# Nearest code by one minimum over 32-bit words of distance and rank

## The chip, the cores and the metric

The kernel runs on one core of a Trainium2 chip. The metric is the device time of one execution in microseconds (us). A core has five engines with instruction queues of their own, each of which works in order: PE (TensorE, matrix multiplication; PEld is its loading of weights), DVE (VectorE), ACT (ScalarE), POOL (GpSimd) and SP (SyncE, which here issues DMAs). [...]

## The reference

A three-tap convolution along time, a SiLU, four stages of residual vector quantisation with eight code words each, and a second three-tap convolution over the sum of the chosen words:

```python
B, T, D, K = 2, 16000, 512, 3
Nq, C = 4, 8
z = sum(xp[:, i:i+T, :] * dw_enc[i] for i in range(K))     # bfloat16
res = silu(z)
for s in range(Nq):
    cb = codebooks[s]
    d2 = |res|^2 - 2 res.cb + |cb|^2                        # [B, T, C]
    idx = d2.argmin(-1)
    sel = cb[idx]
    q = q + sel
    res = res - sel
y = sum(qp[:, i:i+T, :] * dw_dec[i] for i in range(K))
```

`argmin` takes the first of equal distances. The distances are bfloat16, so equal ones do occur, and the kernel has to break ties by the index.

## The kernel before

The 32,000 tokens are cut into 250 groups of 128 tokens (token p*250+g is row p of group g). The groups are worked in 16 chunks: one of 12 groups, fourteen of 16 and one of 14 (`SIZES`, L25). A chunk goes through these steps:

- **load** (L348): one transposing DMA for each group and its two neighbours brings x into XT, with the 512 features on the partitions in four blocks of 128. SP issues it (L358). There are two XT buffers. The first chunk comes another way (`load_rows`, L319), through PE transposes and four moves by ACT and DVE (L335, L337).
- **front** (L383): for each of the four blocks, `product` multiplies by the three taps (L410, into one Z and two T tiles), `total` adds them (L418), then ACT computes exp (L422), DVE adds one (L426), ACT computes the logarithm (L430) and exp (L433), and DVE writes the product into RES (L438). There are three Z tiles, three T tiles and three RES buffers.
- **stage** (L469), four times: PE scores the tokens in three banks of 5 or 6 groups (L489, L494). DVE takes the squared norm as a maximum (L502, TR) and copies the eight dot products (L505, PR). Then comes a tail of six small DVE instructions on 128 partitions x 16 groups x 8 codes, once for each stage and chunk, 64 times in all, each reading what the one before wrote: `with_norm` (L522, V), `distance` (L528, D2), `least` (L532, the minimum M over the eight codes), `marks` (L536: is the distance equal to the minimum?), `first` (L541, the maximum M2) and `onehot` (L549, OH). PE transposes OH (L559), ACT copies it out of PSUM (L566), PE multiplies it with the negated code words (L584), and the result is added to RES by DVE (L596) or, together with a copy of RES through PE (L601), by ACT (L607). How many of the four blocks go by DVE is the list `ON_DVE`.
- **finish** (L664): PE decodes from the four one-hot codes (L633), ACT moves the result out (L639, YSB, three buffers) and SP stores it (L643).

A KEY buffer is a tile of 32-bit words, also viewed as pairs of bfloat16. Before the first use `presets` (L269) writes the rank C-c into the lower half of every word of each of the three buffers, by eight memsets for each (L271). `marks` writes 1 or 0 into the upper half; among the words with a 1 the float32 maximum is then the one with the highest rank, which is the lowest code index. `presets` also clears the OH buffer (L272).

The order on each engine comes from a planner, `Plan` (L40). Every step is a task with an engine, a hold and a delay (assumed costs in us), the tasks that it needs, a due time, and the slots (buffers) that it takes and gives. The planner plays the program through: whenever an engine is free, the ready task with the earliest due time whose slots are there goes next, and its instructions are emitted in that order. Real waits are then set by semaphores that follow the actual reads and writes. In the plan a chunk's XT slot is given back when the third product of the fourth block is done (`give=("XT",)`, L452); the products need only the load. The tail's six tasks stand at L570 to L575 with holds of 0.2, 0.15, 0.2, 0.2, 0.2 and 0.2 us, the presets at L298 with 0.8 us, and the task with `taps_of`, which clears a decoder table on DVE and loads it through POOL's queue (L286, L288), at L303.

Of the kernel before, what the change touches and what calls it, by code (L numbers as in the profile page):

```python
# [10 lines left out]
BF16 = mybir.dt.bfloat16  # L11
F32 = mybir.dt.float32
ALU = mybir.AluOpType
ACT = mybir.ActivationFunctionType
AX = mybir.AxisListType
# [3 lines left out]
GC = 16  # L19
J = 4  # L20
# [99 lines left out]
def kernel(  # L120
# [8 lines left out]
    nc = tc.nc  # L129
    P = nc.NUM_PARTITIONS  # L130
    B, T, D = x.shape
    K = dw_enc.shape[0]
    Nq, C, _ = codebooks.shape
    KT = D // P
# [9 lines left out]
    const = ctx.enter_context(tc.tile_pool(name="const", bufs=1))  # L144
# [5 lines left out]
    small = ctx.enter_context(tc.tile_pool(name="small", bufs=3))  # L150
# [31 lines left out]
    for i in range(KT):  # L182
# [3 lines left out]
    free = {"RES": [], "KEY": [], "OH": []}  # L186
    plan = Plan({"XT": 2, "Z": ZB, "T": TB, "E": EB, "LN": LNB, "Y": YB, "psG": 2, "psD": 2, "psA": 2, "RES": 3, "KEY": 3,
                 "OH": 3})

    RESB = []  # L190
    for n in range(3):
        t = const.tile([P, KT, 2 * GC, NC + HT], BF16, name=f"RES{n}")
# [5 lines left out]
    G = chunks[0]["G"]  # L198
# [4 lines left out]
    for b in range(B):  # L203
        p = b * HB
# [58 lines left out]
    for n in range(3):  # L263
        t = const.tile([P, GC, C], F32, name=f"KEY{n}")
        free["KEY"].append((t, t.rearrange("p g c -> p (g c)").bitcast(BF16).rearrange("p (g c h) -> p g c h", c=C, h=2)))
        t = const.tile([P, GC, Nq, C], BF16, name=f"OH{n}")
        free["OH"].append(t)

    def presets(n):  # L269
        for c in range(C):  # L270
            nc.vector.memset(KEYS[n][1][:, :, c, 0], float(C - c))  # L271
        nc.vector.memset(OHB[n], 0.0)  # L272

    KEYS, OHB = list(free["KEY"]), list(free["OH"])

# [1 line left out]
    for name, first, tap, count in (("A0", 0, 1, 2), ("A1", 0, 0, 3), ("A2", 1, 0, 3), ("A3", 2, 0, 2),  # L279
                                    ("B0", 3, 0, 1), ("B3", 0, 2, 1), ("A2LO", 1, 0, 1)):  # L280
        t = const.tile([P, D], BF16, name=name)
# [16 lines left out]
    preset = [plan.add("DVE", 0.8, 1.0, [], early + 2.0 if n == 0 else 0.1 * PERIOD, lambda n=n: presets(n)) for n in range(3)]  # L298
# [3 lines left out]
    for n, name in enumerate(PARTS):  # L302
        t = plan.add("DVE", 0.2, 6.0, [], (0.3 + 0.02 * n) * PERIOD, lambda name=name: taps_of(name))  # L303
# [79 lines left out]
    def front(st, org):  # L383
        n, G, MB = st["n"], st["GP"], st["MB"]
        f = G / GC

        def dve(full):
            return 0.1 + (full - 0.1) * f

        def act(full):  # L390
            return 0.2 + (full - 0.2) * f


        def taps(i, k):
            return st["XT"][:, i, k:k + G, :].rearrange("p (m j) t -> p j m t", j=J)

        def places(t):
            return t[:, 0:G, :].rearrange("p (j m) t -> p j m t", m=MB)

        def halves(t):  # L400
            return t[:, 0:G, :].rearrange("p n (h t) -> p (n h) t", t=HT)

        def block(i):
            u = {}

            def product(k):
                name = "ZTU"[k]
                u[name] = (zpool if k == 0 else tpool).tile([P, GC, P], BF16, name="Z" if k == 0 else f"T{k}",
                                                            tag="z" if k == 0 else "t")
                nc.vector.tensor_scalar(out=places(u[name]), in0=taps(i, k), scalar1=WENC[:, i, k:k + 1], scalar2=None,  # L410
                                        op0=ALU.mult)

            def total(k):
                z, t = u["Z"][:, 0:G, :], u["ZTU"[k]][:, 0:G, :]
                if k <= DMA_ADDS:
                    nc.gpsimd.dma_start(out=z, in_=t, accum_op=ALU.add)
                else:
                    nc.vector.tensor_tensor(out=z, in0=z, in1=t, op=ALU.add)  # L418

            def exp():  # L420
                u["E"] = epool.tile([P, GC, P], BF16, name="E")
                nc.scalar.activation(u["E"][:, 0:G, :], u["Z"][:, 0:G, :], ACT.Exp, scale=-1.0)  # L422

            def one():
                e = u["E"][:, 0:G, :]
                nc.vector.tensor_scalar(out=e, in0=e, scalar1=1.0, scalar2=None, op0=ALU.add)  # L426

            def log():
                u["LN"] = lnpool.tile([P, GC, P], F32, name="LN")
                nc.scalar.activation(u["LN"][:, 0:G, :], u["E"][:, 0:G, :], ACT.Ln)  # L430

            def inverse():
                nc.scalar.activation(u["E"][:, 0:G, :], u["LN"][:, 0:G, :], ACT.Exp, scale=-1.0)  # L433

            def silu():
                if i == 0:
                    st["RES"] = free["RES"].pop(0)
                nc.vector.tensor_tensor(out=st["RES"][:, i, 0:2 * G, LC:LC + HT], in0=halves(u["Z"]), in1=halves(u["E"]),  # L438
                                        op=ALU.mult)

            due = org + (i * SPREAD - LEAD) * PERIOD

            def add_up(k, needs):
                if k <= DMA_ADDS:
                    return plan.add("ACC", 1.2 + 1.8 * f, 7.5, needs, due, lambda: total(k), give=("T",))
                return plan.add("DVE", dve(1.13), dve(1.13) + 0.1, needs, due, lambda: total(k), give=("T",))

            hold, delay = dve(0.67), dve(0.67) + 0.1
            z = plan.add("DVE", hold, delay, st["loaded"], due, lambda: product(0), take=("Z",))
            t = plan.add("DVE", hold, delay, st["loaded"], due, lambda: product(1), take=("T",))  # L450
            z = add_up(1, [z, t])
            t = plan.add("DVE", hold, delay, st["loaded"], due, lambda: product(2), take=("T",), give=("XT",) if i == KT - 1 else ())  # L452
            st["taps"].append(t)
            z = add_up(2, [z, t])
            e = plan.add("ACT", act(1.8), act(1.8) + 0.12, [z], due, exp, take=("E",))
            e = plan.add("DVE", dve(0.6), dve(0.6) + 0.1, [e], due, one)
            e = plan.add("ACT", act(1.8), act(1.8) + 0.12, [e], due, log, take=("LN",))
            e = plan.add("ACT", act(1.8), act(1.8) + 0.12, [e], due, inverse, give=("LN",))
            r = plan.add("DVE", dve(1.13), dve(1.13) + 0.1, [e] + [t for t in st["silu"][-1:]], due, silu,
                         take=("RES",) if i == 0 else (), give=("Z", "E"))  # L460
            st["silu"].append(r)
            for j in range(J):
                st["new"][i, j] = r

        st["taps"], st["silu"], st["new"] = [], [], {}
        for i in range(KT):
            block(i)

    def stage(st, s, due):  # L469
        G, MB = st["GP"], st["MB"]  # L470
# [3 lines left out]
        u = {}  # L474
# [48 lines left out]
                                    op=ALU.add)  # L523

        def distance():
            u["D2"] = small.tile([P, GC, C], BF16, name="D2")
            g2 = GPOS[:, C * s:C * s + C].rearrange("p (o c) -> p o c", o=1).to_broadcast([P, G, C])
            nc.vector.tensor_tensor(out=u["D2"][:, 0:G, :], in0=u["V"][:, 0:G, :], in1=g2, op=ALU.add)  # L528

        def least():  # L530
            u["M"] = small.tile([P, GC], BF16, name="M")
            nc.vector.tensor_reduce(out=u["M"][:, 0:G], in_=u["D2"][:, 0:G, :], axis=AX.X, op=ALU.min)  # L532

        def marks():
            u["KEY"] = free["KEY"].pop(0)
            nc.vector.tensor_tensor(out=u["KEY"][1][:, 0:G, :, 1], in0=u["D2"][:, 0:G, :],  # L536
                                    in1=u["M"][:, 0:G].to_broadcast([P, G, C]), op=ALU.is_equal)

        def first():
            u["M2"] = small.tile([P, GC], F32, name="M2")  # L540
            nc.vector.tensor_reduce(out=u["M2"][:, 0:G], in_=u["KEY"][0][:, 0:G, :], axis=AX.X, op=ALU.max)  # L541

        def onehot():
            if s == 0:
                st["OH"] = free["OH"].pop(0)
            dst = st["OH"][:, 0:G, s, :].rearrange("p (m j) c -> p j m c", j=J)
            key = u["KEY"][0][:, 0:G, :].rearrange("p (j m) c -> p j m c", m=MB)
            best = u["M2"][:, 0:G].rearrange("p (j m) -> p j m", m=MB).to_broadcast([P, J, MB, C])
            nc.vector.tensor_tensor(out=dst, in0=key, in1=best, op=ALU.is_equal)  # L549
            free["KEY"].append(u["KEY"])  # L550
            if s == Nq - 1 and G > st["G"]:
                nc.vector.memset(st["OH"][:, st["G"]:G, :, :], 0.0)
# [15 lines left out]

        due += 0.01 * PERIOD
        t = plan.add("DVE", 0.2, 0.33, maxima, due, with_norm)  # L570
        t = plan.add("DVE", 0.15, 0.26, [t], due, distance)
        t = plan.add("DVE", 0.2, 0.33, [t], due, least)
        t = plan.add("DVE", 0.2, 0.33, [t] + preset[0:3], due, marks, take=("KEY",))
        t = plan.add("DVE", 0.2, 0.33, [t], due, first)
        t = plan.add("DVE", 0.2, 0.36, [t], due, onehot, take=("OH",) if s == 0 else (), give=("KEY",))  # L575
        t = plan.add("PE", 0.05 + 0.06 * MB, 0.25 + 0.06 * MB, [t], due, turn, take=("psA",), give=("OH",) if s == Nq - 1 else ())
        t = plan.add("ACT", 0.2 + 0.3 * f, 0.32 + 0.3 * f, [t], due, turned, give=("psA",))
# [156 lines left out]
```

## Time and profile before

| What | Value |
|---|---|
| runs | 828.19, 830.86 and 836.56 us; median 830.86 us |
| span of the profiled execution, first to last instruction | 824.6 us (its own time outside the span is not listed; the median run is 6.3 us above the span) |
| busy time in it | DVE 752.2 us, ACT 717.8 us, PE 653.2 us, POOL 7.4 us |
| granted TensorE clock, mean | 0.912 |
| chain that ended last | ACT 41%, DVE 31%, PE 22%, issue 3%, DMA 2% |

A row of the profile names the line, the engine, the operation and what goes in and out, then busy time, the mean duration of one instruction and the engine's idle time before the group. The profile drops buffer numbers and trailing digits, so M and M2 are both M, and D2 is D. DVE instructions overlap: an instruction of 284 ns can be followed by the next one 202 ns after its start. The chain of waits counts a step only up to the start of what follows, so it shows this distance from start to start and not the duration.

### The profile page before, as it was taken

What the parts mean: (1) busy time and instruction counts of PE and PEld (TensorE: products, weight loads), DVE (VectorE), ACT (ScalarE), POOL (GpSimd) and SP (SyncE); (2) the same over time, 40 slices, a digit from 0 to 9 for tenths busy, and PEclk for the clock granted to TensorE, in tenths of its full rate; (3) what the DMA queues carried; (4) which work ended last, traced back from release to release, by engine and by line L of the source; (5) the groups of instructions that cost most, each with busy time, mean ns of one, the idle gap of its engine ahead of it and who ended that gap; (6) DMA issues with size and microseconds to landing.
All of it is one profiled execution on the core that took longest, in us unless ns stands there. A gap on an engine that the chain in (4) does not pass through costs nothing.

```text
span 824.6 us, 23407 instructions
## 1 busy us (share of the span) xinstructions
PE 653.2 (79%) x10289; PEld 314.0 (38%) x10289; DVE 752.2 (91%) x1584; ACT 717.8 (87%) x623; POOL 7.4 (1%) x17
## 2 busy tenths in 40 slices
PE   3047697898788879868888788779898888989995
PEld 2023333443343444424444244334434434334442
DVE  5987999999999999999999999998989999988871
ACT  2659788898999999999999999998989999886564
POOL 1100000000000000000000000000000000000000
PEclk9566877798998999999999999998979999989998
DMA  7442422152452635253716353451615301111132
GB/s 172 48 98 61 86 52 59 34 117 39 109 111 53 136 70 99 59 119 72 160 53 148 59 117 72 89 138 42 135 44 110 98 36 70 52 79 52 79 143 114
DMA packets 156207, 71.82 MB, mean 87 GB/s; under 512 B 147401, under 2 KB 147786, under 8 KB 155978
## 3 DMA queue, kind: packets, MB, share of 16 engines
q1 hardware_dynamic: 155152, 69.64, 35.8%
q8 instruction: 80, 1.31, 0.7%
q0 software_dynamic: 672, 0.43, 0.5%
q10 hardware_dynamic: 282, 0.26, 0.1%
q14 instruction: 21, 0.17, 0.1%
HBM read 2.39 MB, written 32.77 MB: 43 GB/s over the span
## 4 chain that ended last, share of the span: by engine, by line
ACT 41%; DVE 31%; PE 22%; issue 3%; DMA 2%; ACTq 0%; DVEq 0%
ACT RES L607 11%; ACT LN L430 8%; ACT YSB L639 7%; ACT E L422 7%; ACT E L433 7%; DVE Z L418 6%; DVE RES L596 6%; PE PS L494 6%; PE NEW L601 5%; DVE TR L502 4%; DVE RES L438 3%; DVE T L410 3%; PE NEW L584 3%; PE Y L633 3%; PE SEL L584 2%
## 5 line engine op out<-in xcount | busy, mean ns | idle before, releaser
L607 ACT ACTIVATE RES<-NEW 128x1024 bf16<-128x1024 f32 (+1 forms) x238 | 234.7, 1037 | 29.2 <-PE NEW L584 24.6
L494 PE MATMUL PS<-RES 128*64 128x80 bf16 (+1 forms) x8064 | 189.3, 208 | 27.4 <-DVE RES L438 26.7
L596 DVE TENSOR_TENSOR RES<-RES,SEL 128x512 bf16<-128x512 bf16 (+1 forms) x292 | 185.7, 674 | 19.6 <-PE SEL L584 19.2
L494 PEld LDWEIGHTS <-RES 128*64 128x64 bf16 x8064 | 165.6, 119 | 75.5 <-issue 36.8
L601 PE MATMUL NEW<-RES,IDENT 128*128 128x512 bf16 (+1 forms) x476 | 154.2, 408 | 30.8 <-ACT RES L607 27.0
L418 DVE TENSOR_TENSOR Z<-Z,T 128x2048 bf16<-128x2048 bf16 (+1 forms) x128 | 153.7, 1200 | 0.0
L639 ACT ACTIVATE YSB<-Y 128x1024 bf16<-128x1024 f32 (+1 forms) x126 | 128.1, 1042 | 17.8 <-PE Y L633 12.0
L422 ACT ACTIVATE E<-Z 128x2048 bf16<-128x2048 bf16 (+1 forms) x64 | 122.6, 1916 | 16.2 <-DVE Z L418 16.2
L430 ACT ACTIVATE LN<-E 128x2048 f32<-128x2048 bf16 (+1 forms) x64 | 122.3, 1913 | 8.0 <-DVE E L426 8.0
L433 ACT ACTIVATE E<-LN 128x2048 bf16<-128x2048 f32 (+1 forms) x64 | 122.8, 1920 | 0.2
L502 DVE TENSOR_REDUCE TR<-PS 128x5 bf16<-128x320 f32 (+1 forms) x188 | 95.5, 510 | 17.9 <-PE PS L494 17.5
L633 PE MATMUL Y<-A,OHT 128*128 128x512 bf16 x249 | 86.4, 390 | 30.5 <-ACT RES L607 17.2
L584 PE MATMUL SEL<-OHT,CBN 32*128 32x512 bf16 (+1 forms) x292 | 84.4, 397 | 27.3 <-ACT OHT L566 15.5
L584 PE MATMUL NEW<-OHT,CBN 32*128 32x512 bf16 (+1 forms) x476 | 97.8, 407 | 0.0
L410 DVE TENSOR_SCALAR T<-XT,WENC 128x2048 bf16<-128x2048 bf16 (+1 forms) x128 | 93.5, 740 | 0.0
L584 PEld LDWEIGHTS <-CBN 32*128 32x128 bf16 x768 | 35.2, 92 | 149.9 <-issue 144.4
L438 DVE TENSOR_TENSOR RES<-Z,E 128x2048 bf16<-128x2048 bf16 (+1 forms) x64 | 76.9, 1202 | 6.6 <-ACT E L433 4.0
L601 PEld LDWEIGHTS <-IDENT 128*128 128x128 bf16 x476 | 33.7, 99 | 106.0 <-issue 103.8
L489 PE MATMUL PS<-MASK,IDENT 128*128 128x320 bf16 (+1 forms) x188 | 62.6, 333 | 10.4 <-DVE PR L505 10.1
L633 PEld LDWEIGHTS <-OHT 128*128 128x128 bf16 x373 | 32.5, 98 | 70.2 <-issue 46.9
L566 ACT ACTIVATE OHT<-ps_oh 128x512 bf16<-128x512 bf16 (+1 forms) x64 | 39.7, 623 | 17.0 <-PE ps_oh L559 16.9
L633 PE MATMUL Y<-B,OHT 128*128 128x512 bf16 x124 | 47.4, 383 | 0.1
(73 smaller groups left out, 370.9 us busy)
## 6 DMA issues: line engine op xcount, KB each, us to landing
out_dram<-YSB SPq DMA_DIRECT2D x61, 512.0 KB, 3.2
XT<-in_x_dram SPq DMA_TRANSPOSE x267, 2.8
RES<-in_x_dram SPq DMA_DIRECT2D x1, 1664.0 KB, 6.9
out_dram<-YSB SPq DMA_DIRECT2D x1, 384.0 KB, 2.3
out_dram<-YSB SPq DMA_DIRECT2D x1, 256.0 KB
A<-in_dw_dec_dram POOLq DMA_DIRECT2D x2, 96.0 KB, 5.3
CB<-in_codebooks_dram ACTq DMA_DIRECT2D x1, 128.0 KB
A<-in_dw_dec_dram POOLq DMA_DIRECT2D x2, 64.0 KB, 4.8
```

What stands on the lines that cost most here:

```text
L418: nc.vector.tensor_tensor(out=z, in0=z, in1=t, op=ALU.add)
L422: nc.scalar.activation(u["E"][:, 0:G, :], u["Z"][:, 0:G, :], ACT.Exp, scale=-1.0)
L430: nc.scalar.activation(u["LN"][:, 0:G, :], u["E"][:, 0:G, :], ACT.Ln)
L433: nc.scalar.activation(u["E"][:, 0:G, :], u["LN"][:, 0:G, :], ACT.Exp, scale=-1.0)
L494: nc.tensor.matmul(V[h * HT:(h + 1) * HT, r, :], lhsT=half[:, LC:LC + HT], rhs=half[:, lo:hi], start=False, stop=(i == KT - 1), skip_group ...
L502: nc.vector.tensor_reduce(out=u["TR"][:, q:q + m], in_=u["V", q][:, :, own:own + HT], axis=AX.X, op=ALU.max)
L584: nc.tensor.matmul(ps, lhsT=CBN[s][rows, i * P:(i + 1) * P], rhs=u["OHT"][rows, 0:MB, :], start=start, stop=True, skip_group_check=True)
L596: nc.vector.tensor_tensor(out=old, in0=old, in1=u["SEL", i, j][:, 0:W].rearrange("p (m t) -> p m t", t=HT), op=ALU.add)
L601: nc.tensor.matmul(NEW[:, h, 0:W], lhsT=IDENT, rhs=tokens(i, j + h, 1), start=True, stop=False, skip_group_check=True)
L607: nc.scalar.activation(old, u["NEW", i, j][:, :, 0:W].rearrange("p h (m t) -> p h m t", t=HT), ACT.Copy)
L633: nc.tensor.matmul(Y[:, h, :], lhsT=lhs(), rhs=rhs, start=(a == 0), stop=(a == len(terms) - 1))
L639: nc.scalar.activation(u["YSB"][:, k:k + n, :], u[k][:, 0:n, :], ACT.Copy)
```

## The change

The distance goes straight into the upper half of a KEY word. A new step, `ranks`, writes into the lower half 0 - c/8 where the distance is not negative and 1 - c/8 where it is: of two words with equal upper halves the float32 minimum is then the one with the lower code index, whichever the sign. One minimum over the words takes the place of minimum, marks and maximum, and `onehot` compares against it. The presets no longer write ranks into the KEY buffers; the eight values c/8 are put once into a tile RANK by POOL. In the planner the tail has five tasks, each with a hold of 0.2 us, and `distance` waits for the preset tasks where `marks` did. Two lines of `front` change as well: the third product of the fourth block, which gives the XT slot back, now needs all the other products of its chunk.

```diff
     def presets(n):
-        for c in range(C):
-            nc.vector.memset(KEYS[n][1][:, :, c, 0], float(C - c))
         nc.vector.memset(OHB[n], 0.0)
...
+    RANK = const.tile([P, 1, C], BF16, name="RANK")
+    for c in range(C):
+        nc.gpsimd.memset(RANK[:, :, c], c / C)
...
             z = plan.add("DVE", hold, delay, st["loaded"], due, lambda: product(0), take=("Z",))
             t = plan.add("DVE", hold, delay, st["loaded"], due, lambda: product(1), take=("T",))
+            st["taps"] += [z, t]
             z = add_up(1, [z, t])
-            t = plan.add("DVE", hold, delay, st["loaded"], due, lambda: product(2), take=("T",), give=("XT",) if i == KT - 1 else ())
+            t = plan.add("DVE", hold, delay, st["loaded"] + (st["taps"] if i == KT - 1 else []), due, lambda: product(2), take=("T",), give=("XT",) if i == KT - 1 else ())
             st["taps"].append(t)
...
         def distance():
-            u["D2"] = small.tile([P, GC, C], BF16, name="D2")
+            u["KEY"] = free["KEY"].pop(0)
...
-            nc.vector.tensor_tensor(out=u["D2"][:, 0:G, :], in0=u["V"][:, 0:G, :], in1=g2, op=ALU.add)
+            nc.vector.tensor_tensor(out=u["KEY"][1][:, 0:G, :, 1], in0=u["V"][:, 0:G, :], in1=g2, op=ALU.add)
+
+        def ranks():
+            word = u["KEY"][1]
+            nc.vector.scalar_tensor_tensor(out=word[:, 0:G, :, 0], in0=word[:, 0:G, :, 1], scalar=0.0,
+                                           in1=RANK.to_broadcast([P, G, C]), op0=ALU.is_lt, op1=ALU.subtract)
 
         def least():
-            u["M"] = small.tile([P, GC], BF16, name="M")
-            nc.vector.tensor_reduce(out=u["M"][:, 0:G], in_=u["D2"][:, 0:G, :], axis=AX.X, op=ALU.min)
-
-        def marks():
-            u["KEY"] = free["KEY"].pop(0)
-            nc.vector.tensor_tensor(out=u["KEY"][1][:, 0:G, :, 1], in0=u["D2"][:, 0:G, :],
-                                    in1=u["M"][:, 0:G].to_broadcast([P, G, C]), op=ALU.is_equal)
-
-        def first():
-            u["M2"] = small.tile([P, GC], F32, name="M2")
-            nc.vector.tensor_reduce(out=u["M2"][:, 0:G], in_=u["KEY"][0][:, 0:G, :], axis=AX.X, op=ALU.max)
+            u["M"] = small.tile([P, GC], F32, name="M")
+            nc.vector.tensor_reduce(out=u["M"][:, 0:G], in_=u["KEY"][0][:, 0:G, :], axis=AX.X, op=ALU.min)
...
-        t = plan.add("DVE", 0.15, 0.26, [t], due, distance)
+        t = plan.add("DVE", 0.2, 0.33, [t] + preset[0:3], due, distance, take=("KEY",))
+        t = plan.add("DVE", 0.2, 0.33, [t], due, ranks)
         t = plan.add("DVE", 0.2, 0.33, [t], due, least)
-        t = plan.add("DVE", 0.2, 0.33, [t] + preset[0:3], due, marks, take=("KEY",))
-        t = plan.add("DVE", 0.2, 0.33, [t], due, first)
         t = plan.add("DVE", 0.2, 0.36, [t], due, onehot, take=("OH",) if s == 0 else (), give=("KEY",))
```

More of the change, by code (lines that the diff above doesn't have):

```diff
@@ L269, in presets @@
     def presets(n):
-        for c in range(C):
-            nc.vector.memset(KEYS[n][1][:, :, c, 0], float(C - c))
         nc.vector.memset(OHB[n], 0.0)
-    KEYS, OHB = list(free["KEY"]), list(free["OH"])
+    OHB = list(free["OH"])
+    RANK = const.tile([P, 1, C], BF16, name="RANK")
+    for c in range(C):
+        nc.gpsimd.memset(RANK[:, :, c], c / C)
     PARTS = {}
@@ L547, in onehot @@
             key = u["KEY"][0][:, 0:G, :].rearrange("p (j m) c -> p j m c", m=MB)
-            best = u["M2"][:, 0:G].rearrange("p (j m) -> p j m", m=MB).to_broadcast([P, J, MB, C])
+            best = u["M"][:, 0:G].rearrange("p (j m) -> p j m", m=MB).to_broadcast([P, J, MB, C])
             nc.vector.tensor_tensor(out=dst, in0=key, in1=best, op=ALU.is_equal)
```

## The prediction

> **What bounds the kernel now.** I read the page's busy times first, then the stretches of 50 us, then the chain of waits, then the DVE rows by shape. The times below are of the profiled execution, whose span is 824.6 us; what lies around that span is not listed. The median of the runs shown, 830.86 us, is 6.3 us above the span, and I carry those 6.3 us over unchanged: a saving is worked out in the span and taken off the median.
>
> ```profile
> PE 653.2 (79%) x10289; PEld 314.0 (38%) x10289; DVE 752.2 (91%) x1584; ACT 717.8 (87%) x623; POOL 7.4 (1%) x17
> ACT 41%; DVE 31%; PE 22%; issue 3%; DMA 2%; ACTq 0%; DVEq 0%
> ...
> 400.00:450.00 50.00, 41.24 (x718) 20.73 (x718) 50.00 (x103) 49.82 (x43) 0.00 (x0) 1.00 0.48 110
> 450.00:500.00 50.00, 40.45 (x690) 19.69 (x683) 49.52 (x100) 49.34 (x45) 0.00 (x0) 0.97 0.49 101
> 550.00:600.00 50.00, 41.78 (x645) 19.92 (x645) 44.38 (x92) 46.95 (x42) 0.00 (x0) 0.90 0.43 102
> 750.00:800.00 50.00, 48.13 (x771) 21.93 (x766) 39.48 (x100) 34.06 (x38) 0.00 (x0) 1.00 0.24 97
> ```
>
> The reader is to see that DVE is the busiest engine, and yet that the chain runs more through ACT. In the middle both are full (columns: PE, PEld, DVE, ACT, POOL). At 550 us both have gaps, and after 750 us PE is the full one.
>
> How near the two are is seen by adding up a chunk of 16 groups with the steps from start to start that the chain of waits shows. DVE: 16 subtractions (L596) at 0.60, 8 additions (L418) at 1.13, 12 products (L410) at 0.66, 4 each of L438 at 1.13 and L426 at 0.60, 12 maxima at 0.40 to 0.46, 12 copies at 0.11, 4 tails at 1.15: 44.6 us. ACT: 16 L607 and 8 L639 at 0.91, 12 functions at 1.80, 4 L566 at 0.49: 45.4 us. ACT is 0.8 us ahead of DVE, so time taken from DVE in the full stretch is not time taken from the kernel one for one.
>
> **The tail, step by step.** These are the DVE rows by shape (the last number before the bar is the mean duration), and then four pieces of the chain, whose second column is the step to the next start.
>
> ```profile
> L536 DVE TENSOR_TENSOR KEY<-D,M 128x128 bf16<-128x128 bf16 x60 | 17.9, 299 | 0.2
> L549 DVE TENSOR_TENSOR OH<-KEY,M 128x128 bf16<-128x128 f32 x60 | 17.1, 285 | 0.2
> L532 DVE TENSOR_REDUCE M<-D 128x16 bf16<-128x128 bf16 x60 | 16.8, 280 | 0.3
> L541 DVE TENSOR_REDUCE M<-KEY 128x16 f32<-128x128 f32 x60 | 16.7, 279 | 0.1
> L528 DVE TENSOR_TENSOR D<-V,GPOS 128x128 bf16<-128x128 bf16 x60 | 13.2, 220 | 0.3
> ```
>
> ```profile
> 403.97 0.14 DVE D L528
> 404.77 0.19 DVE M L532
> 406.10 0.21 DVE KEY L536
> 406.90 0.20 DVE M L541
> ```
>
> Removed for each stage of a chunk: L528 at 0.14, L532 at 0.20, L536 at 0.21, L541 at 0.20, together 0.75 us. Added: a distance that writes every second half-word, as L536 does, so 0.21; `ranks`; and a minimum over float32 words, the same reading as L541, so 0.20. `with_norm` and `onehot` stay. No row shows an instruction with two operations and two tensors. Its lower bound is the contiguous sum L528 at 0.14; its upper bound is a second pass over 128 elements. The row L528 against L536 prices 64 more steps at 0.07, so a second pass of 128 is 0.14 and the upper bound 0.35 us. I take 0.21, the row whose reading and writing it resembles most (L536). Added: 0.62 us. DVE saves 0.13 us in a tail, 64 x 0.13 = 8.3 us in all; by the bounds of `ranks` 12.8 us or -0.6 us.
>
> [...]
>
> Should a removed instruction be priced by its duration or its step? In the rows L541 lasts 279 ns and the chain goes on after 0.20 us. [...]
>
> What of it lies on the path? I counted the pieces of the chain of waits through the whole span: L528 19 times (2.75 us), L532 17 times (3.44), L536 19 times (4.26), L541 21 times (4.19), 14.6 us together, of about 19 tails out of 64. In their place 19 x 0.62 = 11.8 us. Gain on the path: **2.8 us**. The other 45 tails lie beside ACT or PE work that ends later; there the saving is hidden, up to the 8.3 us of the case where nothing hides it. With the bounds of `ranks` the path gives 4.2 or 0.2 us.
>
> **The presets.** DVE drops 24 memsets (L271). This is the start of the timeline:
>
> ```profile
> 16.54 0.55 DVE L271 MEMSET KEY<- 128x16 bf16 x8
> 18.97 0.94 PE L330 MATMUL ps_x<-IDENT,RES 128*128 128x128 bf16 x14 [1.75 <-ACT XT L337]
> 19.06 2.83 POOL L288 DMA_DIRECT2D A<-in_dw_dec_dram  x4 [17.76 <-DVE A L286]
> 21.25 1.03 DVE L335 COPY XT<-ps_x 128x1792 bf16<-128x1792 bf16 x1
> ```
>
> Three times 0.55 us, all on the chain, 1.65 us. The work behind them on DVE moves up, and with it the clearing of the decoder table (L286) for which POOL's loads wait, so those loads move up too. Late next is the second move, L335 at 21.25: 1.65 us earlier it would come at 19.6, before its transposes end at 19.9 us, which wait for ACT and do not move. So I count **1.3 us** (bounds 0 and 1.65). The eight memsets of RANK go to POOL ahead of its first load. POOL's memsets of 128x1 at the start last 0.10 us, so 0.8 us at most, in the 17.8 us that POOL spends waiting for L286. Without that cover the loads would come 0.8 us later, and DVE's wait for them (L292, 0.48 us now) would grow by as much. The KEY buffer is taken one task earlier; no wait before a KEY instruction is listed, and there are three.
>
> **The XT slot.** The needs added to the third product are the part that is easily overlooked.
>
> ```profile
> SPq L358 <- DVE Z L418: 52.2, 3, 21.6
> ACT YSB L639 <- DMA out_dram<-YSB: 1.1, 1, 1.1
> 599.41 0.50 SPq L643 DMA_DIRECT2D out_dram<-YSB  x1
> 619.00 0.75 DVE L410 TENSOR_SCALAR Z<-XT,WENC 128x2048 bf16<-128x2048 bf16 x1
> 619.77 4.11 SPq L358 DMA_TRANSPOSE XT<-in_x_dram  x3
> ```
>
> SP stops after the store at 599.4 and begins the next chunk's loads at 619.77, just when a first product (Z<-XT) ends at 619.75. So the last reader of the XT buffer was a first product, and the plan had given the slot back some 20 us before: the first product of a block had to wait for a Z tile while the third had its T tile. With the change the plan waits for it. The transfers can't start earlier or later than now, since the real release is the same read. What moves is their place in SP's queue: stores that stood behind the stopped load come ahead of it. All that waits for a store today is one ACT wait of 1.1 us; I count **1.1 us** (bounds 0 and 1.1). On DVE the third product moves behind the first one of its block, and the order of everything after is drawn anew by the planner, which also finds the tail 0.15 us of hold shorter. I cost that redrawing at nothing; what hides it is that DVE and ACT together are full from 300 to 550 us in the present order. Its price if that cover is gone is in the third rival.
>
> **Sum:** 2.8 + 1.3 + 1.1 = 5.2 us off the profiled execution; 830.86 - 5.2 = **825.6 us**, or -0.6%. Its own range, with a second pass in `ranks`, the chain's other bounds and half of the rest hidden or not, is 822 to 830.
>
> **Rivals.**
> *DVE carries all of it.* The planner fills the time that DVE wins and every tail counts: 8.3 + 1.3 + 1.1 = 10.7, which gives 820.2 us, and with `ranks` at 0.14 us 815.7. For it: DVE is the busiest engine by 34 us, and its idle time from 300 to 550 us is 4 us. Against it: ACT's 45.4 us in a chunk.
> *ACT holds the end.* Only the start (1.3) and the last tail gain: it runs from 806.3 to 808.2 us with nothing beside it at 0.24 to 0.34 us a step, so one step, 0.3 us: 829.3 us. For it: 41% of the chain. Against it: DVE pieces stand on the chain all through the middle.
> *The redrawn order is worse, so it is slower.* The plan counts a load of 18 transposes at 2.2 us each, 40 us, and now starts it up to 20 us later in its own time; the front of the chunk after next is then ready late in the plan, and has less time to fill the gaps of PE's scoring. The place is the stretch from 300 to 550 us, where five pieces of 50 us have 0.0 to 2.0 us of DVE idle (4.0 together), while the two after it, with the same work, have 5.6 and 4.0, 4.8 in the mean. If all five become like those two, that costs 5 x 4.8 - 4.0 = 20 us: 845.6 us. It decides from the second such piece (5.2 us are used up by 1.3 of them). Against it: the loads take 1.3 to 1.5 us each in SP's row, not 2.2, and DVE is never listed as waiting for XT.
> The change doing nothing because `ranks` takes two passes is the first sum with 0.2 in place of 2.8: 828.3 us; it belongs to the forecast's own range.
>
> **How the numbers follow.** My forecast has 0.45; DVE carrying all 0.26; ACT holding the end 0.11; the worse order 0.18. One per cent is about what a measurement here can tell from no change, 8.3 us, so faster means below 822.6 and slower above 839.2. Of the forecast 0.04 falls below 822.6. Faster: 0.26 + 0.04 = 0.30; same: 0.41 + 0.11 = 0.52; slower: 0.18. The range reaches from 815 (all of DVE, with the cheap `ranks`) to 841, inside the worse order, which is cut at about half of its chance; some 0.15 is left out.
>
> **What would show it.** DVE's row for `ranks` should read about 300 ns, the distance about 300 and not 220, and the tail five rows; DVE's busy sum falls by about 10 us (8.3 and 1.65). The first product of the first chunk should start at 21.8 and not at 23.1 us. SP's waits for DVE at L358 should lose their 20 us. A `ranks` row above 400 ns, a first product at 23 us, or a list of DVE waits in which L410 waits for an XT transfer would each break one of the steps. The sum fails if the stretch from 300 to 550 us shows more than 10 us of DVE idle, or if ACT's idle there falls to nothing with DVE's rising, which is the second rival.

## The result and the profile after

| | us |
|---|---|
| before, median (range) | 830.14 (828.19 to 836.56) |
| changed kernel, median (range) | 841.93 (838.41 to 842.92) |
| ratio, 95% interval | 1.0156 [1.0121, 1.0190] |
| span, before and after | 824.6 and 836.6 |

The changed kernel is 1.6% slower. Ratios leave out disturbed executions and are not taken from the medians, so a ratio is not always that of the medians beside it. The page and the DVE rows by shape of the changed kernel, where the tail's new lines are L532, L537 and L542:

```profile
PE 668.0 (80%) x10227; PEld 318.3 (38%) x10293; DVE 745.1 (89%) x1496; ACT 718.9 (86%) x623; POOL 6.9 (1%) x25
ACT 38%; DVE 29%; PE 25%; issue 4%; DMA 2%; SPq 0%; ACTq 0%; DVEq 0%
```

```profile
L537 DVE SCALAR_TENSOR_TENSOR KEY<-KEY,RANK 128x128 bf16<-128x128 bf16 x60 | 17.8, 297 | 0.3
L532 DVE TENSOR_TENSOR KEY<-V,GPOS 128x128 bf16<-128x128 bf16 x60 | 17.8, 297 | 0.3
L542 DVE TENSOR_REDUCE M<-KEY 128x16 f32<-128x128 f32 x60 | 16.6, 276 | 0.2
```

The instructions cost what was forecast: `ranks` lasts 297 ns, and the next one starts 202 ns (median) after it. DVE is 7 us less busy, and the kernel still takes 12 us more. DVE's idle time (span less busy time) grew from 72.4 to 91.5 us; between 300 and 700 us alone it grew from 15.6 to 35.8 us. The four stretches from 500 us of the changed kernel (columns as before; PEclk is the number after the five engines):

```profile
500.00:550.00 50.00, 43.41 (x634) 19.86 (x639) 43.26 (x88) 43.10 (x38) 0.00 (x0) 0.83 0.32 81
550.00:600.00 50.00, 40.65 (x645) 19.76 (x651) 44.71 (x89) 48.22 (x43) 0.00 (x0) 0.97 0.43 95
600.00:650.00 50.00, 43.32 (x566) 18.07 (x570) 41.16 (x82) 41.17 (x38) 0.00 (x0) 0.80 0.28 75
650.00:700.00 50.00, 44.88 (x684) 20.31 (x685) 42.65 (x86) 44.60 (x39) 1.62 (x4) 0.83 0.24 73
```

In three of the four DVE and ACT have gaps of 5 to 9 us, PE is the fullest engine although it runs fewer matmuls (from 600 to 650 us 566 against 646 before; this trace lacks some matmul records, and the weight loads say 570 against 645), and the granted clock is low (0.83, 0.80 and 0.83). Before the change three of these stretches read:

```profile
500.00:550.00 50.00, 41.25 (x701) 20.03 (x699) 49.24 (x107) 48.63 (x43) 0.00 (x0) 1.00 0.45 88
600.00:650.00 50.00, 42.18 (x646) 19.20 (x645) 45.97 (x94) 47.37 (x41) 2.01 (x4) 0.90 0.38 96
650.00:700.00 50.00, 43.43 (x711) 20.32 (x711) 48.04 (x101) 48.95 (x44) 0.00 (x0) 0.97 0.11 44
```

There the clock was at 1.00, 0.90 and 0.97, and DVE and ACT were the fuller engines.

### The profile page after: what moved, and what is told of

Same layout as the page of the kernel before. It is cut to its first block, busy times and chain, and to the rows that moved or that the text cites. A ratio compares the mean times of both kernels' runs of the same rounds, so it can differ in the third digit from the quotient of the medians.

```text
span 836.6 us, 23272 instructions
## 1 busy us (share of the span) xinstructions
PE 668.0 (80%) x10227; PEld 318.3 (38%) x10293; DVE 745.1 (89%) x1496; ACT 718.9 (86%) x623; POOL 6.9 (1%) x25
## 4 chain that ended last, share of the span: by engine, by line
ACT 38%; DVE 29%; PE 25%; issue 4%; DMA 2%; SPq 0%; ACTq 0%; DVEq 0%
ACT RES L607 9%; ACT YSB L639 8%; ACT LN L433 7%; PE NEW L601 6%; PE PS L498 6%; DVE RES L596 6%; ACT E L425 6%; ACT E L436 6%; DVE Z L421 6%; PE NEW L584 4%; DVE RES L441 3%; DVE T L413 3%; DVE TR L506 3%; PE Y L633 3%; PE SEL L584 3%
## 5 line engine op out<-in xcount | busy, mean ns | idle before, releaser
L498 PE MATMUL PS<-RES 128*64 128x80 bf16 (+1 forms) x8064 | 191.7, 209 | 29.5 <-DVE RES L441 28.3
L596 DVE TENSOR_TENSOR RES<-RES,SEL 128x512 bf16<-128x512 bf16 (+1 forms) x292 | 185.2, 672 | 26.5 <-PE SEL L584 26.2
L498 PEld LDWEIGHTS <-RES 128*64 128x64 bf16 x8064 | 167.6, 119 | 76.9 <-issue 35.8
L601 PE MATMUL NEW<-RES,IDENT 128*128 128x512 bf16 (+1 forms) x476 | 159.7, 421 | 31.0 <-ACT RES L607 27.9
L639 ACT ACTIVATE YSB<-Y 128x1024 bf16<-128x1024 f32 (+1 forms) x126 | 126.9, 1036 | 19.6 <-PE Y L633 12.6
L433 ACT ACTIVATE LN<-E 128x2048 f32<-128x2048 bf16 (+1 forms) x64 | 121.8, 1904 | 13.7 <-DVE E L429 13.6
L584 PE MATMUL SEL<-OHT,CBN 32*128 32x512 bf16 (+1 forms) x292 | 88.3, 411 | 22.1 <-DVE RES L596 10.9
L633 PE MATMUL Y<-A,OHT 128*128 128x512 bf16 x227 | 81.6, 391 | 28.3 <-ACT RES L607 13.9
L584 PE MATMUL NEW<-OHT,CBN 32*128 32x512 bf16 (+1 forms) x476 | 101.0, 421 | 0.0
L584 PEld LDWEIGHTS <-CBN 32*128 32x128 bf16 x768 | 34.7, 93 | 147.4 <-issue 143.5
L601 PEld LDWEIGHTS <-IDENT 128*128 128x128 bf16 x476 | 33.6, 99 | 114.2 <-issue 111.9
L493 PE MATMUL PS<-MASK,IDENT 128*128 128x320 bf16 (+1 forms) x188 | 63.3, 336 | 12.5 <-DVE PR L509 11.5
L413 DVE TENSOR_SCALAR Z<-XT,WENC 128x2048 bf16<-128x2048 bf16 (+1 forms) x64 | 47.0, 735 | 0.0
```

Of the source, the lines that this page charges most:

```text
L498: nc.tensor.matmul(V[h * HT:(h + 1) * HT, r, :], lhsT=half[:, LC:LC + HT], rhs=half[:, lo:hi], start=False, stop=(i == KT - 1), skip_group ...
L584: nc.tensor.matmul(ps, lhsT=CBN[s][rows, i * P:(i + 1) * P], rhs=u["OHT"][rows, 0:MB, :], start=start, stop=True, skip_group_check=True)
L596: nc.vector.tensor_tensor(out=old, in0=old, in1=u["SEL", i, j][:, 0:W].rearrange("p (m t) -> p m t", t=HT), op=ALU.add)
L601: nc.tensor.matmul(NEW[:, h, 0:W], lhsT=IDENT, rhs=tokens(i, j + h, 1), start=True, stop=False, skip_group_check=True)
L633: nc.tensor.matmul(Y[:, h, :], lhsT=lhs(), rhs=rhs, start=(a == 0), stop=(a == len(terms) - 1))
L639: nc.scalar.activation(u["YSB"][:, k:k + n, :], u[k][:, 0:n, :], ACT.Copy)
```

## The experiments

### Instructions or order?

Theory: the order drawn anew by the planner costs the time, not the instructions. Rival: the instructions themselves cost it, by a wait that their rows don't show. The planner can be given the old tail tasks and still emit the new instructions, and the other way round, so that PE, ACT and SP keep their order exactly. `new_in_old`, against the changed kernel:

```diff
-            st["taps"] += [z, t]
-            t = plan.add("DVE", hold, delay, st["loaded"] + (st["taps"] if i == KT - 1 else []), due, lambda: product(2), ...
+            t = plan.add("DVE", hold, delay, st["loaded"], due, lambda: product(2), ...
-        t = plan.add("DVE", 0.2, 0.33, [t] + preset[0:3], due, distance, take=("KEY",))
+        t = plan.add("DVE", 0.15, 0.26, [t], due, distance)
         t = plan.add("DVE", 0.2, 0.33, [t], due, ranks)
-        t = plan.add("DVE", 0.2, 0.33, [t], due, least)
+        t = plan.add("DVE", 0.2, 0.33, [t] + preset[0:3], due, least, take=("KEY",))
+        t = plan.add("DVE", 0.2, 0.33, [t], due, lambda: None)
```

> The changed instructions in the order of before: the planner is given the six tail tasks of before with their holds (one of them emits nothing, the ranks step and the one minimum stand in the places of the first minimum and the marks), and the added needs of the third product are left out, so PE, ACT and SP have the very instruction order of before. Theory 'the order costs it': the instructions save what the prediction summed for the path and the start, 4 to 10 us, 820 to 826 us where before has 830. Rival 'the instructions cost it' (ranks, or the half-word writes, wait longer than their rows tell): 838 us or more. Rival 'ACT holds the end': 828 to 830 us.

`old_in_new` is the kernel before with the added needs and five tail tasks of 0.2 us, one of which emits `marks` and `first`:

> The instructions of before in the order of the changed kernel: five tail tasks of 0.2 us, one of which emits both the marks and the maximum, and the added needs of the third product; PE, ACT and SP have the very order of the changed kernel. 'The order costs it': 842 us plus the 4 to 10 us that the instructions save, 846 to 852 us. 'The instructions cost it': about 830 us, as before.

`b_taps` is the kernel before with only the two lines of `front` from the change:

> The kernel before with nothing but the added needs of the third product of the fourth block. Theory 'the late XT slot costs it': 840 to 852 us, with DVE idle in the middle of the span as in the changed kernel (20 us more than before over the whole span). Rival 'the shorter tail in the plan redraws the order for the worse': 828 to 832 us, no change.

`new_in_old_taps` is `new_in_old` with these two lines:

> The changed instructions with the added needs, but with six tail tasks and the holds of before in the plan; PE, ACT and SP have the order of the kernel of before with the added needs. 'The late XT slot costs it': 838 to 846 us, like the changed kernel. 'The shorter tail redraws the order': 820 to 828 us. Whatever the order costs, it should lie 4 to 10 us below the run with the same order and the old instructions.

Measured, median in us and ratio to the kernel before, which was run again beside each set:

| order of PE, ACT and SP | old instructions | new instructions |
|---|---|---|
| of before | 828.4 | 823.0, 0.9946 [0.9910, 0.9982] |
| added needs only | 854.5, 1.0297 [1.0246, 1.0348] | 850.6, 1.0259 [1.0208, 1.0310] |
| added needs and shorter tail (the change) | 849.3, 1.0245 [1.0189, 1.0301] | 841.9, 1.0156 [1.0121, 1.0190] |

In each row the new instructions save 4 to 7 us. The rival falls. Two runs came out slower than expected: `b_taps` at 854.5 us where 840 to 852 was written, and `new_in_old_taps` at 850.6 where 838 to 846 was written, 3.9 us below the old instructions in that order. The added needs cost 26 us with the old instructions, and the shorter tail in the plan takes some of that back (5 us with the old instructions, 9 with the new). So the sum's gain is there, and the loss sits in the part that the prediction had costed at nothing.

### Is it the load, late in the plan?

The prediction's third rival gave a mechanism: the XT slot comes back later, the plan counts 40 us for a chunk's loads, and the next fronts are late. `b_lategive` separates the slot from the product: the third product stays free, and a task without instructions gives the slot back when all twelve products are done.

```diff
-... lambda: product(2), take=("T",), give=("XT",) if i == KT - 1 else ())
+... lambda: product(2), take=("T",))
+            if i == KT - 1:
+                plan.add("NOTE", 0.0, 0.0, st["taps"], due, lambda: None, give=("XT",))
```

> The kernel before, where the third product of the fourth block stays as free as it was and only the XT slot is given back later: by a task without instructions and without time that needs all twelve products of the chunk. Theory 'the late slot (and so the late load and front in the plan) costs it': like the run with the added needs, 848 to 856 us. Rival 'the third product's later place on DVE costs it': 826 to 834 us.

`a_fast` is the changed kernel with `plan.add("SP", 1.4, 1.4, ...)` for a load in place of 1.4 and 2.2, `a_notaps_fast` the same without the added needs. (The changed kernel without the added needs and at 2.2 us was not run; I expect its queues to wait for each other, which no run shows.)

> The changed kernel with one number changed: a transposing load is ready after 1.4 us in the plan, not after 2.2, so that a chunk's 18 loads take 25 us of plan and not 40. The traces show 1.3 to 1.5 us between loads that nothing holds up. 'The late load in the plan costs it': most of the 20 us comes back, 818 to 828 us. Rival 'the real transfers are late, the plan is not the cause': 838 to 845 us, or slower with waits of DVE for XT transfers.

> The changed kernel without the added needs of the third product, and with 1.4 us for a load in the plan: the nearest to the tail's change alone, since without the added needs and at 2.2 us the queues lock each other and it can't be tried. 'The late slot costs it': 815 to 826 us. Rival 'every new order is worse than the one of before': 835 us or more.

And `b_hold` is a mere redrawing, 0.2 and 0.33 for the distance task in the kernel before:

> The kernel before with 0.2 us and 0.33 us for the distance task in the plan in place of 0.15 and 0.26, which draws the whole order anew and leaves instructions and needs as they are. It shows how far a mere redrawing moves the time. Theory 'only the late slot is bad': 826 to 834 us. Rival 'the order of before is a lucky one and any other is worse': 838 us or more.

Measured: `b_lategive` 836.0 us with runs from 822 to 842, 1.003 [0.997, 1.008], too uncertain to use (the ratio rests on four of its ten executions, and the median of all ten is 1.0% above the 827.7 us of the kernel before beside it); `a_fast` 851.2 us, 1.028 [1.023, 1.034]; `a_notaps_fast` 853.3 us, 1.030 [1.025, 1.035]; `b_hold` 835.3 us, 1.0095 [1.0056, 1.0134], between its two expectations. With quicker loads in the plan it gets worse, and it is as bad without the added needs. So my theory of the late load falls. These two orders also differ early (the first product of one chunk, near 170 us, comes 67 and 64 us after that of the chunk before it, where all later ones come within 59), so they do not tell what is bad about the changed order. The mere redrawing cost 1%.

### The clock of PE

The next theory came from setting the runs side by side by granted clock: PE pauses, its clock is halved, and everything waits for PE. The rival is the order alone, with the clock only following. The trace's record of it has two values, 1.0 and 0.5, in stretches that are multiples of 3.41 us. The sum of the 0.5 stretches from 300 to 700 us, against the span of the profiled execution (one for each kernel):

| kernel | half clock, us | span, us |
|---|---|---|
| before | 31 | 824.6 |
| new_in_old | 38 | 817.6 |
| b_hold | 41 | 832.4 |
| b_lategive | 51 | 834.2 |
| old_in_new | 72 | 844.7 |
| the changed kernel | 75 | 836.6 |
| a_fast | 85 | 847.5 |
| b_taps | 92 | 851.9 |
| new_in_old_taps | 102 | 851.6 |
| a_notaps_fast | 102 | 849.6 |

How a stretch begins can be read in PE's timeline of the changed kernel:

```profile
600.91 0.40 PE L560 MATMUL ps_oh<-IDENT,OH 128*128 128x128 bf16 x4
601.15 0.49 PE L316 MATMUL PS<-MASK,IDENT 128*128 128x384 bf16 x2
604.14 0.47 PE L584 MATMUL SEL<-OHT,CBN 32*128 32x512 bf16 x2 [2.51 <-ACT OHT L567]
604.54 1.03 PE L601 MATMUL NEW<-RES,IDENT 128*128 128x512 bf16 x2
```

PE pauses for 2.51 us until ACT has copied the one-hot codes. At 604.3 the clock drops for 17.1 us, and the pair of matmuls L601 takes 1.03 us. At the full clock it takes 0.60. The two other long drops, at 501.9 for 13.7 us and at 655.5 for 17.1, follow the same wait (1.20 and 1.42 us). Through all of the long stretches PE is 98 to 100% busy: there it is the bound, and DVE and ACT wait for it (DVE's subtractions, L596, waited 3.7, 5.7 and 3.8 us for PE's products, L584, in the three). Fillers (L313 before, L316 after) are meant to bridge such pauses; the planner counts 0.3 us for one, but four in a row take 0.81 us, of which the last has 0.33, so 0.16 from start to start.

How much of the loss is at half clock? From 300 to 700 us DVE was idle for 15.6 us before, 8.1 of them in the half-clock stretches, and is idle for 35.8 us in the changed kernel, 19.6 of them there. So 11.5 of the 20 us more lie in half-clock stretches, and the rest, near 9 us, at the full clock. Whether that rest is the new order's own cost or an after-effect of the half clock, the trace does not tell.

Which is cause? With the order of DVE, ACT and SP kept, only fillers are taken away or multiplied; they write a bank that is written again later. `b_nofill` is the kernel before without them; `a_fill3` the changed kernel with each three times; `a_mask3` the changed kernel with the mask matmul ahead of each bank three times; `nio_fill2` is `new_in_old` with fillers doubled.

```diff
     def warm():
...
-        nc.tensor.matmul(pending[0]..., lhsT=IDENT, rhs=MASK, start=True, stop=True, ...)
+        for _ in range(3):
+            nc.tensor.matmul(pending[0]..., lhsT=IDENT, rhs=MASK, start=True, stop=True, ...)
```

> The kernel before in its very order on DVE, ACT and SP, but the planner's filler matmuls on PE (L313, 100 of them, which only rewrite a bank that is written again later) are not emitted. The granted clock of the runs so far has two values, 1.0 and 0.5; from 300 to 700 us it is 0.5 for 31 us in the kernel before, 75 in the changed kernel, 92 in the one with the added needs alone, and PE is busy all through those stretches, so half of each is lost to PE. Theory 'the clock': without fillers PE pauses more, the half-clock time grows past 60 us and the time to 838 to 850 us. Rival 'the order alone': 822 to 829 us, since PE only loses work.

> The changed kernel in its very order on DVE, ACT and SP, but each of its filler matmuls is issued three times (200 more on PE, about 0.16 us each at the full clock, 33 us of PE). 'The clock': the half-clock time from 300 to 700 us falls from 75 to below 50 us and the time from 842 to 825 to 837 us. Rival 'the order alone': 842 us or more, because PE has more to do.

> The changed kernel in its very order on DVE, ACT and SP, but the mask matmul that opens each bank of scores (188 of them) is issued three times: 376 more, 50 to 60 us of PE, each just ahead of the place where PE waits for RES. 'The clock': the half-clock time in the middle goes to 0 to 30 us; the gain of up to 25 us is set against the longer PE, 822 to 840 us. 'The order alone': 850 us or more.

> The changed instructions in the order of before, with each filler matmul issued twice: is there a version that beats both? 'The clock': of the 37 us of half clock from 300 to 700 us some go, 813 to 822 us where the same without more fillers had 823. 'The order alone': 823 us or more.

Measured: `b_nofill` 839.1 us, 1.0126 [1.0087, 1.0166], half clock 75 us, as 'the clock' expected; `a_fill3` 829.9 us, 1.0015 [0.9971, 1.0059], half clock 26 us, also as expected; `a_mask3` 836.5 us, 1.0087 [1.0057, 1.0117], half clock 34 us, where 0 to 30 us was written, but within its 822 to 840 us; `nio_fill2` 823.9 us, 0.9943 [0.9913, 0.9972], half clock 51 us, a miss: 813 to 822 us and less half clock than 38 was written. The changed kernel's order gets 12 us back by adding work to PE, and the order of before loses 10 to 12 us by taking work away; the order alone explains neither. The clock alone does not explain everything either. `new_in_old`, with the same instructions in the order of before, has a ratio of 0.9946; the change stands at 1.0156 and `a_fill3` at 1.0015, so more fillers bring back two thirds of what the order costs, though over its ten executions `a_fill3` has a mean clock of 0.935 where the kernel before has about 0.912. And `b_nofill` with a mean clock of 0.866 is faster than `b_taps` with 0.871 by 14 us. The clock, mean of each of 40 slices, in the changed kernel, in `a_fill3`, in the kernel before and in `b_nofill`:

```profile
PEclk9566795997988989989999996999969698999999
```

```profile
PEclk9579996998799999998999999999999988999999
```

```profile
PEclk9566877798998999999999999998979999989998
```

```profile
PEclk9555667898798896969799889988999798978998
```

The sixes of the changed kernel's second half are gone in `a_fill3`, and `b_nofill` has them in its middle, where the kernel before has nines. In `a_fill3` the wait for the one-hot codes that is shown above ends at about the same place, after a pause of 1.09 us, and leaves no drop of the clock behind:

```profile
599.94 1.14 PE L317 MATMUL PS<-MASK,IDENT 128*128 128x384 bf16 x6
602.17 0.39 PE L585 MATMUL SEL<-OHT,CBN 32*128 32x512 bf16 x2 [1.09 <-ACT OHT L568]
602.50 0.60 PE L602 MATMUL NEW<-RES,IDENT 128*128 128x512 bf16 x2
```

`a_mask3` shows the other side: it puts 15 us more on PE from 300 to 700 us, its half clock gathers after 550 us, and it wins 5 us where `a_fill3` wins 12; which of the two takes the rest is not separated. `nio_fill2` has more half clock from 300 to 700 us than `new_in_old` in the one execution that was traced of each, a higher mean clock over all executions (0.924 against 0.904), and the same time: small differences of the clock do not rank the kernels. Of the versions run, `new_in_old` and `nio_fill2` beat both kernels, by 0.5% over the one before.

### What was left open

`bt_fill3` is `b_taps`, the costliest order, with fillers three times; `b_lategive2` is `b_lategive` again with more rounds.

> The kernel before with the added needs of the third product (the run at 854 us), in its very order on DVE, ACT and SP, each filler matmul issued three times. 'The clock': the added needs cost what they do by PE's pauses, so most of the 26 us comes back, 828 to 840 us, and the half-clock time from 300 to 700 us falls from 92 to below 55 us. Rival 'the late slot itself starves DVE and ACT, the clock only follows': 848 us or more.

> The run with the XT slot given back late and the third product left free, once more with more rounds, because its interval held both no change and 0.8%. If the late slot alone makes PE pause: a ratio of 1.02 to 1.03. If the third product's place on DVE does: 0.997 to 1.01.

Measured: `bt_fill3` 833.1 us, 1.0051 [1.0020, 1.0081], half clock 32 us in place of 92: 21 of the 26 us that the added needs cost come back, as 'the clock' expected. The other 5 do not, though the mean clock of its twelve executions is 0.945, above the 0.912 of the kernel before; whether the order or the added fillers cost them is not separated. From 300 to 700 us, `b_taps` and then `bt_fill3`:

```profile
300.00:700.00 400.00, 341.81 (x5176) 159.61 (x5175) 362.65 (x740) 368.13 (x318) 1.63 (x4) 0.88 0.38 88
```

```profile
300.00:700.00 400.00, 341.63 (x5440) 167.47 (x5481) 376.44 (x770) 380.55 (x332) 1.63 (x4) 0.96 0.39 92
```

PE is as busy as it was and runs 264 matmuls more, 87 of them fillers; DVE and ACT get 14 and 12 us more done in the same 400 us. `b_lategive2` came to 837.5 us, 1.0104 [1.0069, 1.0139], half clock 44 us: between the two expectations, nearer to the rival. The late slot alone costs some 1%. The other 2% of `b_taps` comes with the third product's later place, alone or together with the late slot: the later product by itself was not run. Why these places on DVE make PE pause where they do stays open: the runs show the pauses and what they cost, not a rule for which order has them.

## Why the prediction was wrong, point by point

- *The tail.* Right. `ranks` taken at 0.21 us measured 0.202 from start to start, the distance 0.202 where 0.21 was written, the minimum 0.196. A second pass in `ranks`, my estimate of 0.35 us from L528 and L536 (0.14 and 0.21 us), did not show. The sum rightly takes the time from start to start and not the duration: before the change L541 lasted 279 ns and the next instruction started 196 ns after it did; `ranks` lasts 297 ns. DVE's busy time fell by 7.1 us where about 10 was written (8.8 in `new_in_old`).
- *What of it lies on the path.* Right within the noise, in the order of before. `new_in_old` saves 5.4 us in the medians, and its interval, 0.9910 to 0.9982, is 1.5 to 7.5 us. SP's order, and with it the wait for a store, is that of before there, so the part of the sum that it tests is 2.8 + 1.3 = 4.1 us; that 5.4 lies so near the whole sum of 5.2 is luck. The chain of waits of its profiled execution has 10.6 us in the three new steps, where 14.6 stood in the four old ones and 11.8 was forecast. The first rival, DVE carrying all of it (10.7 us), lies outside the interval even without its 1.1 us for the stores; the second, ACT holding the end (1.6 us), lies at its edge and is not quite excluded.
- *The presets.* Right: the first product starts at 22.44 in place of 23.10 us, while the code words that open DVE's work came 0.57 us later in that execution (9.88 in place of 9.31), so 1.2 us; 1.3 were counted. `new_in_old` gives 1.2 us too (22.01, with the code words at 9.45).
- *The stores.* ACT's wait of 1.1 us for a store is no longer listed in the changed kernel (in `new_in_old` it is, with 1.6 us); what that was worth by itself no run shows. SP's waits for DVE at its loads, which I expected to lose their 20 us, are still there, 133 us in all in place of 173, the longest 20.7 us. And a product of DVE once waits for an XT transfer, for 1.5 us at 46 us, which I had named as a sign that a step is broken. The loads are not the reason: the new order begins that chunk's products at 43.4 us in place of 47.5. The wait is too small to be the loss.
- *The redrawing "costed at nothing".* This is the step that failed. "DVE and ACT together are full from 300 to 550 us in the present order" is a property of that order and no cover for another. In its place the runs show that the added needs cost 26 us by themselves, five times the whole gain, and that the shorter tail moves the time as well; 21 of the 26 us come back with more fillers, at 32 us of half clock in place of 92. Why this order makes PE pause stays open.
- *The third rival* had the sign and the place (DVE's idle time from 300 to 550 us went from 4 to 14 us, past the 10 that I named as the sum's failure), but not the mechanism. It put the loss on loads late in the plan; a plan with shorter loads was no better. That its 845.6 us lies near the measured 841.9 is luck. The two stretches from 550 to 650 us that it took as the price of a bad order were already the half clock: 0.90 in each, against 0.99 from 300 to 550, and 6.9 of their 9.7 us of DVE idle lie in two half-clock stretches of 10.2 us, from 552.7 and from 600.5 us, in which PE was 96 and 100% busy.

```profile
300.00:550.00 250.00, 206.20 (x3533) 101.88 (x3531) 245.98 (x511) 246.01 (x214) 0.00 (x0) 0.99 0.45 97
550.00:700.00 150.00, 127.40 (x2001) 59.44 (x2001) 138.40 (x285) 143.27 (x125) 2.01 (x4) 0.92 0.31 81
```

These two lines are of the kernel before. The column of the clock stands in the prediction's first view as well, 0.90 from 550 to 600 us; the prediction gives it no price.

## What to carry to other kernels

When a planner or a scheduler sets the order, a change to one task's cost or needs is a change to the whole order: measure the new instructions in the old order and the old instructions in the new one before judging either. Look at the granted clock stretch by stretch, and not at busy time alone: here three pauses of PE of 1.2 to 2.5 us were each followed by 14 to 17 us at half clock, in which PE was the bound, while its busy time over the whole span was 79 and 80%. A cheap filler in the pause can be worth more than the instruction saved elsewhere: fillers gave the changed kernel 12 us back, and the shorter tail saves 4 to 7. But they gave nothing in the order of before (`nio_fill2`), so this too has to be measured.

## What the hardware showed beside that

- In the changed kernel the half clock lasted up to 17.1 us (five steps of 3.41 us) with PE 100% busy. The return to the full clock took one to five steps from 300 to 700 us, and in the two longest stretches PE was busy through all five.
- The pauses ahead of the three long drops were 1.20 to 2.51 us, shorter than a step. PE was 27 to 54% busy in the 3.41 us ahead of them, and 27 to 70% ahead of all nine drops from 300 to 700 us. So no whole step was idle ahead of a drop. Three other steps, at 51 to 55%, were followed by none, so no threshold comes out of this trace.
- What a microsecond of half clock is worth, net of the fillers that were added or left out: 61 us less of it went with 21 us (`bt_fill3`), 50 us less with 12 (`a_fill3`), 44 us more with 10 to 12 (`b_nofill`), about a quarter to a third of a microsecond for each. The fillers' own cost is in these figures, so they do not give the price of the clock alone.
